# Holding stores behind a load, joining two sums and reordering products at the start of a fused attention and feed-forward kernel

## The chip, the cores and the metric

The kernel runs on one core of a Trainium2 chip. The metric is device microseconds of one execution. All runs compared here are fast (granted TensorE clock 0.998 to 1.000). PE is TensorE, ACT is ScalarE, DVE is VectorE, POOL is GpSimd, SP is SyncE, which here only issues DMAs. Times "at 47.6 us" count from the first instruction of the profiled execution; the span of a profile is about 1.7 us shorter than the run's measured time. A load "lands" at the time for which the profile shows it complete.

## The reference, cut to what matters

```python
B, H, S, D = 8, 8, 576, 64            # batch, heads, tokens, head size
kv  = einsum('bhsd,bhse->bhde', k, v)
out = einsum('bhsd,bhde->bhse', q, kv)
out = out / sqrt(mean(out*out, -1) + 1e-6) * g_norm
x   = out.transpose(0, 2, 1, 3).reshape(4608, 512)
a, b = x @ w_a, x @ w_b               # 512 -> 1536
return (a * b) @ w_out                # 1536 -> 512
```

All inputs are float32 in HBM. The loads that POOL issues cast to bfloat16.

## The kernel before

The 4608 tokens are worked off in nine strips of 512. A strip's feed-forward part is twelve units, each with a product for a and one for b (four matmuls each), then four output groups of 128 tokens. Attention of batch 0 is done at the start, that of batch 1 between the output groups of strip 0, that of batch n+1 inside strip n. The parts that matter:

```python
def load_late(b):                      # batch 2 and later, issued by POOL
    # ... (a gate against qT's earlier use, for b > 2)
    for hs in (slice(0, NP), slice(NP, H)):
        nc.gpsimd.dma_start(out=d[:, hs, :], in_=q[b, hs]...)   # q to a bf16 scratch qs
    load_heads(b, kt[b % NB], k, slice(0, H))
    load_heads(b, vt[b % NB], v, slice(0, H))

def transpose_q(b):                    # issued by SP
    nc.sync.dma_start_transpose(qT[b % 2], qs_d[b])

def o_out(s, g, i):                    # an output group: PSUM -> o_sb -> HBM
    # ... copy by ACT or DVE into t = o_sb[n % 4]
    store(s * STRIP + g * 128, t, 0, d_model)      # SP, two DMAs as a rule

# order of POOL's loads: batch 0; w_a, w_b; w_out; batch 1 pair by pair; batch 2
    for p in range(NP):
        load_pair(1, p)                # q, k, v of two heads
    load_late(2)

# strip 0's output groups and batch 1's attention
    ffn_o(0, 0, X[0])
    pieces = [(1, h1), (1, h2), (2, h1), (2, h2), (3, h1), (3, h2)]
    for n, (g, fcs) in enumerate(pieces):
        o_mm(0, g, O, fcs)
        if fcs is h2:
            o_out(0, g, O)
        # ... sums, x of earlier pairs
        if n < NP:
            A.qtr(n, 2)                # transpose q of pair n on PE
            A.kv1(n, 2)                # k-v product of pair n: needs kt, vt of pair n
        # ...
    transpose_q(2)
```

Inside strip 1, after unit 4, stands the k-v product of batch 2 (`A.kv`, 48 small matmuls); it needs batch 2's k and v:

```python
def slot(A, s, n):
    k0, kn, xs = (4, 1, (6, 9, 11, 13)) if s < 3 else (2, 1, (4, 7, 10, 12))
    # k-v product after unit k0; x of pair p after unit xs[p]
```

PE works its products off in program order here, so one whose v has not landed holds up what stands behind it (in the run gate_only below it waits 0.82 us, and the next unit starts only after it, at 60.99 us). SP does the same with its DMAs: behind the gate of the change the first store went out at 47.84 us, not at 39.15.

Of the kernel before, what the change touches and what calls it, by code (L numbers as in the profile page):

```python
# [9 lines left out]
BF16 = mybir.dt.bfloat16  # L10
# [5 lines left out]
def kernel(  # L16
# [11 lines left out]
    nc = tc.nc  # L28

    B, H, S, D = q.shape  # L30
# [4 lines left out]
    FC = d_ff // 128  # L35
# [6 lines left out]
    EC, EP = 6, 96  # L42
    EARLY = 2
    KORD = tuple(range(KC))
# [4 lines left out]
    def sb(shape, dt, name):  # L49
        return pool.tile(shape, dt, name=name, tag=name)  # L50

    wa_t = sb([128, KC, d_ff], BF16, "wa_t")
    wb_t = sb([128, KC, d_ff], BF16, "wb_t")
# [7 lines left out]
    vt = [sb([EP, H, EC, D], BF16, f"vt{i}") for i in range(NB)]  # L61
# [27 lines left out]
    O = 3  # L89

    qs_d = {b: tc.dram_tile([S, d_model], BF16, name=f"qs{b}") for b in range(EARLY, B)}

    ctx.enter_context(tc.manual_schedule())

# [129 lines left out]
    class Unit:  # L224
# [19 lines left out]
            self.mm(wa_t, kcs)  # L244
            self.mm(wb_t, kcs)

        def rest(self, kcs=KORD):
            self.mm(wa_t, kcs)
            nc.scalar.copy(self.t, self.a)  # L249
            self.mm(wb_t, kcs)  # L250
            nc.vector.tensor_mul(abt[self.s % 2][self.fc], self.b, self.t)  # L251

    n_ab = [0]

    def ffn_ab(s, fc):
        i = n_ab[0]
        n_ab[0] += 2
        Unit(s, fc, i % 3, (i + 1) % 3).rest()
# [18 lines left out]
    def o_mm(s, g, i, fcs, e0=0, e1=d_model):  # L277
        for fc in fcs:
            nc.tensor.matmul(  # L279
                P[:, i, e0:e1],  # L280
                lhsT=abt[s % 2][fc][:, g * 128 : (g + 1) * 128],
                rhs=wo_t[:, fc, e0:e1],
                start=(fc == 0),
                stop=(fc == FC - 1),
            )

    def o_out(s, g, i):
        n = n_o[0]
        n_o[0] += 1
        t = o_sb[n % 4]  # L290
        if n % 2:
            nc.scalar.copy(t, P[:, i, :])  # L292
        else:
            nc.vector.tensor_copy(t, P[:, i, :])  # L294
        store(s * STRIP + g * 128, t, 0, d_model)

    def ffn_o(s, g, i=O):
        o_mm(s, g, i, range(FC))
        o_out(s, g, i)


    def dummy(n, i, cols=STRIP):
        for _ in range(n):
            nc.tensor.matmul(
                P[:, i, 0:cols], lhsT=zeros[:, 0:128], rhs=zeros[:, 0:cols], start=True, stop=True
            )
# [54 lines left out]
    for p in range(1, NP):  # L361
        i = X[p % 2]
        A.kv1(p, 3 - p % 2)
        A.kv1_out(p, 3 - p % 2, nc.vector.tensor_copy)
        A.pss(p - 1, SS)
        if p < NP - 1:
            dummy(1, 2 + p % 2)
            A.qtr(p + 1, 3 - p % 2)
            A.qtr_out(p + 1, 3 - p % 2)
            A.pst(p - 1, X[(p - 1) % 2])  # L370
            A.px(p, i)
            A.psq(p, i)
            dummy(1 if p == 1 else 2, 2 + p % 2)
# [5 lines left out]
    u1 = Unit(0, 1, 4, 5)  # L379
    u0.first((0, 1))  # L380
    A.pss(3, SS, (0,))
    A.pst(3, X[1], (0,))
    u1.first((0, 1))
    A.pss(3, SS, (1,))
    A.pst(3, X[1], (1,))
    u0.first((2,))
    u1.first((2,))
    u0.rest((3,))
    u1.rest((3,))
    for fc in range(2, FC):  # L390
        ffn_ab(0, fc)


    A = Attn(1)
    h1, h2 = range(0, FC // 2), range(FC // 2, FC)
    ffn_o(0, 0, X[0])
    pieces = [(1, h1), (1, h2), (2, h1), (2, h2), (3, h1), (3, h2)]
    for n, (g, fcs) in enumerate(pieces):
# [16 lines left out]
    u1 = Unit(1, 1, 4, 5)  # L415
# [89 lines left out]
```

## Time and profile before

| What | Value |
|---|---|
| time, median of 6 runs | 323.04 us (322.75 to 323.34) |
| span of the profile | 321.4 us |
| PE busy | 98% |
| start step of 512-column matmuls | 0.216 us |
| PE stalls after 17.6 us | 0.32 us at 44.9, 0.28 us at 47.7 |

From the page of the kernel before: span, busy time of the engines, and the chain that ended last.

```profile
span 321.4 us, 4834 instructions
...
PE 315.2 (98%) x1946; PEld 151.2 (47%) x1946; DVE 123.7 (38%) x214; ACT 125.4 (39%) x216; POOL 60.3 (19%) x82
...
PE 84%; DMA 9%; POOL 4%; issue 1%; ACT 0%; POOLq 0%
```

The chain of waits of the kernel before, from 38 to 62 us (start, duration, what):

```profile
39.98 0.63 POOL kt L97
40.61 0.11 issue
40.72 6.89 DMA vt<-in_v_dram
47.62 0.04 issue
47.66 0.38 PE P L138 x12
...
51.47 8.63 PE P L235 x40
60.10 0.88 PE P L138 x48
```

The last load of batch 1's v, issued at 40.72 us, lands at 47.62 us, and what ends last hangs on it. Before it the chain is made of loads and of POOL's issuing them, after it of PE alone. So there are two regimes: up to 47.6 us the loads set the pace, from then on PE does. A PE bar that is 98% busy doesn't tell of this; the chain does.

The timeline of PE (start, duration, instruction, in brackets idle time and what ended it) and of SP's queue, kernel before:

```profile
17.52 0.38 PE L235 MATMUL P<-xt,wa_t 128*128 128x512 bf16 x1 [0.28 <-DVE xt L203]
...
44.89 0.38 PE L138 MATMUL P<-vt,kt 96*64 96x64 bf16 x12 [0.16 <-DMA vt<-in_v_dram]
...
47.66 0.38 PE L138 MATMUL P<-vt,kt 96*64 96x64 bf16 x12
...
60.03 0.95 PE L138 MATMUL P<-vt,kt 96*64 96x64 bf16 x48
```

```profile
39.15 13.50 SPq L272 DMA_DIRECT2D out_dram<-osb  x8
52.83 6.48 SPq L125 DMA_TRANSPOSE qT<-qs  x1
```

The brackets count from the modelled end of the matmul before, so they are smaller than the true loss. I take the loss from start-to-start steps: the one at 44.89 costs 0.32 us, the one at 47.66 (no bracket at all) 0.28 us, the one at 17.52 0.44 us. The line at 60.03 us is batch 2's product: it did not wait, since its v had landed at 59.46 us.

### The profile page before, as it was taken

Reading aid. Unit: us, or ns where it says so; the run is one execution under the profiler, and the core shown is the slowest. Engines: PE = TensorE matmul, PEld = TensorE weight load, DVE = VectorE, ACT = ScalarE, POOL = GpSimd, SP = SyncE. Lnnn points to the kernel's source line nnn. Section 1 sums busy time; section 2 is a strip of 40 time slices with the busy share of each in tenths; the row PEclk is TensorE's granted clock in tenths of the full one; section 3 lists DMA queues with packets and bytes.
Section 4 is the critical chain, followed back from the end, with each engine's and each line's share of the span. In section 5 each row is a group of like instructions: output and inputs, shape, how many; then the busy total and the mean of one; then the engine's idle time right before and its main releaser. Section 6 shows DMA issues by size and latency. Waiting matters only on the chain.

```text
span 321.4 us, 4834 instructions
## 1 busy us (share of the span) xinstructions
PE 315.2 (98%) x1946; PEld 151.2 (47%) x1946; DVE 123.7 (38%) x214; ACT 125.4 (39%) x216; POOL 60.3 (19%) x82
## 2 busy tenths in 40 slices
PE   7999999999999999999999999999999999999995
PEld 3444454444444444444444445444444444444443
DVE  3543344344234423452244423532354243313421
ACT  3643155453345433552355325433453233123310
POOL 8854970330041230500050000000000000000000
PEclk9999999999999999999999999999999999999999
DMA  8999999796369899693598152003000200020002
GB/s 177 197 196 199 199 219 217 115 144 108 94 95 159 121 168 228 64 168 86 140 98 125 65 90 50 2 33 99 2 0 0 100 33 0 26 91 18 0 35 98
DMA packets 69899, 32.61 MB, mean 101 GB/s; under 512 B 43636, under 2 KB 65396, under 8 KB 69876
## 3 DMA queue, kind: packets, MB, share of 16 engines
q0 software_dynamic: 49712, 18.44, 48.7%
q1 hardware_dynamic: 19808, 13.44, 16.2%
q10 hardware_dynamic: 356, 0.43, 0.5%
q8 instruction: 15, 0.25, 0.3%
q14 instruction: 8, 0.07, 0.1%
HBM read 37.75 MB, written 12.98 MB: 158 GB/s over the span
## 4 chain that ended last, share of the span: by engine, by line
PE 84%; DMA 9%; POOL 4%; issue 1%; ACT 0%; POOLq 0%
PE P L235 52%; PE P L279 27%; DMA wb_t<-in_moe_w_b_dram 6%; DMA vt<-in_v_dram 2%; PE P L189 2%; PE P L215 2%; PE P L138 2%; DMA qt<-in_q_dram 2%; POOL wo_t L112 1%; POOL qt L97 1%; POOL kt L97 1%; POOL vt L97 1%; POOL wa_t L332 0%; POOL wb_t L332 0%; POOL wa_t L108 0%
## 5 line engine op out<-in xcount | busy, mean ns | idle before, releaser
L251 DVE TENSOR_TENSOR ab<-P,asb 128x512 bf16<-128x512 f32 x108 | 74.5, 691 | 124.1 <-PE P L235 123.1
L235 PE MATMUL P<-xt,wa_t 128*128 128x512 bf16 x432 | 111.9, 379 | 0.3 <-DVE xt L203 0.3
L235 PE MATMUL P<-xt,wb_t 128*128 128x512 bf16 x432 | 111.8, 379 | 0.0
L279 PE MATMUL P<-wo_t,ab 128*128 128x512 bf16 (+1 forms) x444 | 97.9, 373 | 0.0
L249 ACT CAST asb<-P 128x512 bf16<-128x512 f32 x108 | 63.0, 585 | 81.5 <-PE P L235 80.0
L235 PEld LDWEIGHTS <-wb_t 128*128 128x128 bf16 x432 | 42.3, 98 | 51.4 <-issue 0.6
L279 PEld LDWEIGHTS <-ab 128*128 128x128 bf16 x444 | 43.1, 98 | 45.6
L235 PEld LDWEIGHTS <-wa_t 128*128 128x128 bf16 x432 | 41.7, 98 | 44.2 <-issue 0.2
L203 DVE SCALAR_TENSOR_TENSOR xt<-P,g_col,rs 128x288 bf16<-128x288 f32 x64 | 30.2, 513 | 25.0 <-ACT rs L193 25.0
L193 ACT ACTIVATE rs<-P,eps_t 128x576 f32<-128x576 f32 (+1 forms) x33 | 24.0, 727 | 22.4 <-PE P L189 18.4
L292 ACT COPY osb<-P 128x512 f32<-128x512 f32 x17 | 9.9, 585 | 48.6 <-PE P L279 46.8
L185 ACT ACTIVATE sq<-P 128x576 bf16<-128x576 f32 x31 | 20.2, 650 | 20.0 <-PE P L215 18.0
L294 DVE COPY osb<-P 128x512 f32<-128x512 f32 x18 | 12.4, 691 | 32.8 <-PE P L279 32.8
L120 POOL DMA_DIRECT2D qs<-in_q_dram x12 | 19.5, 1633 | 1.8 <-issue 1.7
L117 POOL COPY gate<-qT 1x1 bf16<-1x1 bf16 x5 | 0.9, 177 | 92.4 <-DMA qT<-qs 92.4
L189 PE MATMUL P<-sq,ones 128*128 128x288 bf16 x64 | 13.3, 286 | 0.5 <-ACT sq L185 0.4
L215 PE MATMUL P<-qT,kvb 128*128 128x288 bf16 x56 | 11.7, 286 | 0.0
L149 ACT CAST kvb<-P 64x256 bf16<-64x256 f32 (+1 forms) x20 | 6.0, 301 | 11.8 <-PE P L138 11.7
L189 PEld LDWEIGHTS <-ones 128*128 128x128 bf16 x64 | 6.2, 98 | 7.5 <-issue 0.4
L138 PEld LDWEIGHTS <-kt 96*64 96x64 bf16 x384 | 7.4, 112 | 4.3 <-issue 3.9
L97 POOL DMA_DIRECT2D vt<-in_v_dram x13 | 9.1, 697 | 0.7 <-DMA qt<-in_q_dram 0.5
L97 POOL DMA_DIRECT2D kt<-in_k_dram x13 | 9.1, 704 | 0.1
(41 smaller groups left out, 65.5 us busy)
## 6 DMA issues: line engine op xcount, KB each, us to landing
out_dram<-osb SPq DMA_DIRECT2D x23, 256.0 KB, 2.0
qs<-in_q_dram POOLq DMA_DIRECT2D x12, 288.0 KB, 6.6
kt<-in_k_dram POOLq DMA_DIRECT2D x6, 576.0 KB, 8.4
vt<-in_v_dram POOLq DMA_DIRECT2D x6, 576.0 KB, 11.0
out_dram<-osb SPq DMA_DIRECT2D x13, 128.0 KB, 2.3
wo_t<-in_moe_w_out_dram POOLq DMA_DIRECT2D x12, 128.0 KB, 6.0
wa_t<-in_moe_w_a_dram POOLq DMA_DIRECT2D x5, 256.0 KB, 9.3
wb_t<-in_moe_w_b_dram POOLq DMA_DIRECT2D x5, 256.0 KB, 9.9
```

The lines of the kernel that those rows point to most:

```text
L97: nc.gpsimd.dma_start(out=t[:, hs, :, :], in_=src[b, hs].rearrange("h (t c) d -> t h c d", c=EC))
L120: nc.gpsimd.dma_start(out=d[:, hs, :], in_=q[b, hs].rearrange("h t d -> t h d"))
L138: nc.tensor.matmul(o[j * D : (j + 1) * D, :], lhsT=kt[self.b % NB][:, 2 * p + j, c, :], rhs=vt[self.b % NB][:, 2 * p + j, c, :], start=(c ...
L185: nc.scalar.activation(sq[p % 3], P[:, i0 : i0 + 2, 0:HF], AF.Square)
L189: nc.tensor.matmul(P[:, i0 + h, 0:HF], lhsT=ones, rhs=sq[p % 3][:, h, :], start=True, stop=True)
L193: nc.scalar.activation(rs[p % 3][:, h0:h1, :], P[:, i0 + h0 : i0 + h1, 0:HF], AF.Abs_reciprocal_sqrt, bias=eps_t,)
L203: nc.vector.scalar_tensor_tensor(out=xt[p][:, t0 : t0 + HF], in0=P[:, x0 + h, 0:HF], scalar=g_col, in1=rs[p % 3][:, h, :], op0=ALU.mult, o ...
L215: nc.tensor.matmul(P[:, i0 + h, 0:HF], lhsT=kvb[self.b % 2][:, p, :], rhs=self.qT[:, p, h * HF : (h + 1) * HF], start=True, stop=True,)
L235: nc.tensor.matmul(self.a if w is wa_t else self.b, lhsT=w[:, kc, self.fc * 128 : (self.fc + 1) * 128], rhs=xt[kc][:, t0 : t0 + STRIP], st ...
L249: nc.scalar.copy(self.t, self.a)
L251: nc.vector.tensor_mul(abt[self.s % 2][self.fc], self.b, self.t)
L279: nc.tensor.matmul(P[:, i, e0:e1], lhsT=abt[s % 2][fc][:, g * 128 : (g + 1) * 128], rhs=wo_t[:, fc, e0:e1], start=(fc == 0), stop=(fc == F ...
```

## The change

The intent: (1) keep the stores of strip 0 from competing with the loads of batch 1, by putting a one-element store ("the gate") that reads the last element of batch 1's last v load ahead of them on SP; (2) put the two halves' sums of pair 3 close together, so that the second half is not late; (3) do a of units 2 and 3 before their b, since w_b lands later; (4) drop a filler matmul (`dummy`, which multiplies zeros).

In the code `kc` counts the four chunks of 128 that the 512 channels of x are cut into. The weights of units 0 and 1 are loaded two chunks at a time, so their w_b comes as one load for kc 0-1, below "the first w_b chunk", and one for kc 2-3. `pss` sums the squares on PE and takes the reciprocal root on ACT, `pst` scales to x on DVE.

```diff
+    gate_d = tc.dram_tile([1, 1], BF16, name="gate_d")
...
         if p < NP - 1:
-            dummy(1, 2 + p % 2)
+            if p == 1:
+                dummy(1, 2 + p % 2)
...
     u0.first((0, 1))
     A.pss(3, SS, (0,))
     A.pst(3, X[1], (0,))
-    u1.first((0, 1))
+    u1.mm(wa_t, (0,))
     A.pss(3, SS, (1,))
     A.pst(3, X[1], (1,))
+    u1.mm(wa_t, (1,))
+    u1.mm(wb_t, (0, 1))
     u0.first((2,))
     u1.first((2,))
     u0.rest((3,))
     u1.rest((3,))
-    for fc in range(2, FC):
+
+    u2 = Unit(0, 2, 0, 1)
+    u3 = Unit(0, 3, 2, 0)
+    u2.part_a()
+    u3.part_a()
+    u2.part_b()
+    u3.part_b()
+    n_ab[0] = 1
+    for fc in range(4, FC):
         ffn_ab(0, fc)
...
+    nc.sync.dma_start(out=gate_d, in_=vt[1][0:1, H - 1, EC - 1, D - 1 : D])
     ffn_o(0, 0, X[0])
```

(`rest` is split into `part_a` and `part_b`; the cut lines only do that.)

More of the change, by code (lines that the diff above doesn't have):

```diff
@@ L245, in first, with part_a, part_b, rest @@
             self.mm(wb_t, kcs)
-        def rest(self, kcs=KORD):
+        def part_a(self, kcs=KORD):
             self.mm(wa_t, kcs)
             nc.scalar.copy(self.t, self.a)
+        def part_b(self, kcs=KORD):
             self.mm(wb_t, kcs)
             nc.vector.tensor_mul(abt[self.s % 2][self.fc], self.b, self.t)
+        def rest(self, kcs=KORD):
+            self.part_a(kcs)
+            self.part_b(kcs)
     n_ab = [0]
```

## The prediction

> **What bounds the kernel now.** The page gives PE 98% busy of a 321.4 us span; in the timeline 512-column matmuls start every 0.216 us. After 17.6 us PE stalls only twice: at 44.89 us (0.32 us) and 47.66 us (0.28 us), when the k-v product of batch 1's pairs 2 and 3 waits for v (landings 44.85 and 47.62 us). The chain of waits agrees: up to 47.6 us it runs through POOL's DMA issues and landings, afterwards through PE alone. So until 47.6 us loads are the bound and PE has small slack; afterwards PE bounds.
>
> **What the change does.**
> 1. *Removed dummy (p = 2).* 0.21 us, because the square/rsqrt chain on ScalarE has about that slack.
> 2. *Sums of pair 3 together.* PE idled 0.44 us before 17.52 us: the second half's sum was issued at 16.09, its rsqrt ended 16.91, its scaling 17.47 us. One matmul instead of four between the sums brings that sum some 0.65 us forward; the wait goes, but the w_b chunk for kc 2-3, landing 16.26 us, then bites for about 0.1 us. Estimate: the last quarter of units 0 and 1 starts near 17.05 us, not 17.52.
> 3. *a of units 2, 3 before b.* w_b for unit 2 lands at 18.91 us and would stall the advanced PE by about 0.25 us; after the swap it is needed near 19.6. Cost: unit 4's a reuses unit 2's b bank one product group (0.86 us) after it, while its 0.69 us multiply with hand-over takes about 1.0 us: 0.15 us lost. Net at unit 4: 0.3 us ahead.
> 4. *Gate.* A one-element store waits for batch 1's last v load, so the two stores of strip 0's first two token groups (issued 39.15 to 42.9 us, 512 KB) cannot move beside the loads. The Trainium skill ("DMA: Bandwidth & Descriptors", Issuing engines are not separate DMA queues) says that transfers from all issuers interleave on the same 16 engines. This trace agrees: load traffic fell from 195 to 130-140 KB/us at 42-44 us while stores moved 115-137; load landings slipped from 0.74 us apart to 1.0-1.3.
>
> **On the critical path.** The 0.3 us of the first part is mostly absorbed: pair 0's v lands at 39.70 us whatever PE does, pair 0's product started at 39.90, so only 0.16 us survives; pair 1 (41.95 against 42.11) leaves 0.12. With stores held, v of pairs 2 and 3 should land near 44.15 and 46.4 us, both waits vanish, and pair 3's product starts near 46.9 instead of 47.66: 0.75 us ahead. But the bytes are only postponed: the stores now meet batch 2's loads. Its v landed at 59.46 us and its product started at 60.03, so if that landing stays put, only about 0.5 us remains. PE carries the rest to the end.
>
> **Prediction:** 322.6 us (0.5 us, 0.15%, less), range 322.0 to 323.2. Faster by over 2%: 0.01; within: 0.98; slower: 0.01.
>
> **Right if:** no PE gap near 17.5; pair 0's product waits for v at about 39.7 us; pair 3's v lands before 46.7 us; no store issue between 39 and 46 us; PE shows no wait at pairs 2 and 3; batch 2's product starts 59.3 to 59.6 us, possibly waiting for v.
>
> **Wrong if:** the released stores and the transpose of batch 2's q delay batch 2's v beyond 60.0 us (then same or slower); landings shift between runs by more than the 0.1-0.2 us margins.

## The result, and the profile after

The changed kernel took 323.32 us, median of 6 runs (322.45 to 324.26); before took 323.04 (322.75 to 323.34). The ratio is 1.0011, with a 95% interval of 0.9992 to 1.0031: the same. (Ratios here are the mean time of one kernel's fast runs over that of the other's of the same rounds, so not quite the ratio of the medians.) The predicted 322.6 us and its range, up to 323.2, were missed. Mark the scatter too: 1.8 us against 0.6 us.

The page after:

```profile
span 322.5 us, 4835 instructions
...
PE 80%; DMA 14%; POOL 4%; issue 1%; ACT 0%; POOLq 0%
```

The chain of waits after, up to 80 us, and the timelines of PE and SP's queue:

```profile
45.35 0.77 POOL kt L99
46.12 15.04 DMA vt<-in_v_dram
61.15 0.04 issue
61.20 0.95 PE P L140 x48
```

```profile
15.71 0.60 PE L237 MATMUL P<-xt,wb_t 128*128 128x512 bf16 x2 [1.05 <-DMA wb_t<-in_moe_w_b_dram]
...
45.32 0.36 PE L140 MATMUL P<-vt,kt 96*64 96x64 bf16 x12
...
47.78 0.35 PE L140 MATMUL P<-vt,kt 96*64 96x64 bf16 x12
...
61.20 0.95 PE L140 MATMUL P<-vt,kt 96*64 96x64 bf16 x48 [1.00 <-DMA vt<-in_v_dram]
```

```profile
47.50 0.29 SPq L416 DMA_DIRECT2D gate_d<-vt  x1
47.84 5.12 SPq L280 DMA_DIRECT2D out_dram<-osb  x8
53.59 6.66 SPq L127 DMA_TRANSPOSE qT<-qs  x1
```

Three things are to be seen. The waits that the change aimed at, at 17.5, 44.9 and 47.7 us, are gone. But the last two are not gone because v came early: in this execution pair 3's v landed at 47.49 us, hardly before the 47.62 of the kernel before, and PE, late by 0.76 us at pair 0 (40.66 against 39.90 us), asked for it only at 47.78. A new wait stands at 15.7 us: the first w_b chunk landed at 15.66 us, not at 14.00. And the load regime now ends at 61.2 us, not at 47.6: the chain hangs on batch 2's v, which landed at 61.15 us instead of 59.46. The product of batch 2 lost 1.07 us start to start (it began 1.38 us after the matmul before it, 0.31 us in the kernel before). The whole difference of the two spans, 322.5 less 321.4, is there: 61.20 less 60.03.

### The profile page after: what moved, and what is told of

It reads as the page before. It is cut to its first block, busy times and chain, and to the rows that moved or that the text cites. A ratio compares the mean times of both kernels' runs of the same rounds, so it can differ in the third digit from the quotient of the medians.

```text
span 322.5 us, 4835 instructions
## 1 busy us (share of the span) xinstructions
PE 315.1 (98%) x1945; PEld 151.1 (47%) x1945; DVE 123.6 (38%) x214; ACT 125.3 (39%) x216; POOL 60.2 (19%) x82
## 4 chain that ended last, share of the span: by engine, by line
PE 80%; DMA 14%; POOL 4%; issue 1%; ACT 0%; POOLq 0%
PE P L237 49%; PE P L287 26%; DMA wb_t<-in_moe_w_b_dram 6%; DMA vt<-in_v_dram 5%; PE P L217 2%; PE P L191 2%; DMA wo_t<-in_moe_w_out_dram 2%; PE P L140 2%; DMA qt<-in_q_dram 2%; POOL qs L122 1%; POOL kt L99 1%; POOL vt L99 1%; POOL qt L99 1%; POOL wa_t L340 0%; POOL wb_t L340 0%
## 5 line engine op out<-in xcount | busy, mean ns | idle before, releaser
L191 PE MATMUL P<-sq,ones 128*128 128x288 bf16 x64 | 13.2, 286 | 0.5 <-ACT sq L187 0.4
L140 PE MATMUL P<-vt,kt 96*64 96x64 bf16 x384 | 8.6, 197 | 1.0 <-DMA vt<-in_v_dram 1.0
```

What stands on the lines that cost most here:

```text
L140: nc.tensor.matmul(o[j * D : (j + 1) * D, :], lhsT=kt[self.b % NB][:, 2 * p + j, c, :], rhs=vt[self.b % NB][:, 2 * p + j, c, :], start=(c ...
L191: nc.tensor.matmul(P[:, i0 + h, 0:HF], lhsT=ones, rhs=sq[p % 3][:, h, :], start=True, stop=True)
```

## The experiments

Theory A: the gate only postpones the stores. All 1 MB of them now meets the load of batch 2, whose v then lands after its product is due. Rival B: the late w_b chunk, a matter of chance, and what follows from it. Rival C: the changed start itself costs time. The table has all runs; "wait" is what the brackets of the PE timeline show at batch 2's product, and "b1 v" and "b2 v" are the landings of the last v load of batches 1 and 2.

| Run | median us (range) | ratio to before, interval | b1 v, us | b2 v, us | wait, us |
|---|---|---|---|---|---|
| again | 323.41 (322.59 to 324.52) | 1.0012, 0.9995 to 1.0028 | 47.59 | 60.83 | 0.55 |
| gate_only | 323.17 (322.46 to 323.63) | 1.0001, 0.9988 to 1.0014 | 46.20 | 60.06 | 0.82 |
| no_gate | 323.03 (322.69 to 323.25) | 0.9999, 0.9987 to 1.0011 | 47.47 | 59.54 | none |
| late_slot | 324.08 (323.79 to 324.32) | 1.0031, 1.0019 to 1.0043 | 46.29 | 60.49 | none |
| late2 | 322.55 (322.15 to 323.26) | 0.9985, 0.9972 to 0.9998 | 46.31 | 59.29 | none |
| gate_late2 | 322.82 (322.56 to 323.44) | 0.9997, 0.9983 to 1.0011 | 46.39 | 60.03 | none |
| gate2 | 322.45 (322.41 to 323.01) | 0.9984, 0.9972 to 0.9997 | 46.35 | 56.43 | none |
| hold_transpose | 323.59 (323.26 to 323.68) | 1.0013, 1.0000 to 1.0027 | 46.22 | 59.51 | 0.22 |
| before_late2 | 323.25 (322.84 to 323.57) | 1.0002, 0.9990 to 1.0014 | 47.60 | 59.94 | none |
| after_gate2 | 322.35 (322.22 to 322.75) | 0.9976, 0.9963 to 0.9989 | 46.34 | 56.73 | none |
| again2 | 322.63 (322.36 to 323.79) | 0.9991, 0.9972 to 1.0009 | 46.41 | 59.67 | 0.32 |
| before_again | 323.03 (322.50 to 323.12) | 0.9993, 0.9978 to 1.0007 | 47.53 | 59.47 | none |
| wb_late_after | 323.48 (323.35 to 324.03) | 1.0015, 1.0002 to 1.0029 | 46.37 | 59.95 | none |
| wb_late_before | 323.60 (323.19 to 324.06) | 1.0016, 1.0003 to 1.0028 | 47.10 | 59.07 | none |

None of these differences comes near 2%. The intervals tell more, but among fourteen of them one that misses 1 by a hair (late2, gate2) proves little by itself. Each trace is one execution.

### The changed kernel again, and its two halves

`again` has no edit. `gate_only` is the kernel before with the two gate lines of the diff; `no_gate` is the changed kernel without them.

> The changed kernel once more, unaltered. Theory A (the gate moves 1 MB of stores into the load of batch 2, so that batch 2's v lands after its product is due): v of batch 2 lands later than 60.3 us again and PE stands about 0.3 to 1.2 us before the product of strip 1; time within 0.5 us of before, spread over 1 us. Rival B (chance: in the profiled run the first w_b chunk happened to land at 15.66 us instead of 14.00 and everything after it is a consequence): with w_b landing near 14.0 the PE wait at 15.7 is gone, v of batch 2 lands near 59.5, and the time is 0.5 us or more under before.

> The kernel before with nothing but the gate. Theory A: v of batch 2 lands at 60.3 to 61.5 us and PE waits for it; batch 1's pairs 2 and 3 do not wait; time equal to before or up to 0.7 us above. Rival B (gate harmless and useful): batch 1's last v at 46.4 us, batch 2's v near 59.5 us, time 0.3 to 0.6 us under before.

> The changed kernel without the gate: only the start is changed. Theory A: v of batch 2 lands near 59.5 us and the product of strip 1 does not wait, batch 1's pairs 2 and 3 wait for v as before; time 0 to 0.3 us under before, since loads absorb what the start gains. Rival C (the changed start itself costs time, PE waiting for the first w_b chunk): time above before, with the loss still there at 47 us.

The PE timelines of no_gate and of gate_only, and gate_only's SP queue:

```profile
39.73 0.38 PE L139 MATMUL P<-vt,kt 96*64 96x64 bf16 x12
...
44.91 0.38 PE L139 MATMUL P<-vt,kt 96*64 96x64 bf16 x12 [0.30 <-DMA vt<-in_v_dram]
...
59.88 0.95 PE L139 MATMUL P<-vt,kt 96*64 96x64 bf16 x48
```

```profile
46.87 0.35 PE L139 MATMUL P<-vt,kt 96*64 96x64 bf16 x12
...
60.11 0.95 PE L139 MATMUL P<-vt,kt 96*64 96x64 bf16 x48 [0.82 <-DMA vt<-in_v_dram]
```

```profile
46.22 0.29 SPq L397 DMA_DIRECT2D gate_d<-vt  x1
46.55 5.58 SPq L273 DMA_DIRECT2D out_dram<-osb  x8
53.73 6.24 SPq L126 DMA_TRANSPOSE qT<-qs  x1
```

The gate does what it was made for: batch 1's v lands at 46.20 us and pair 3's product starts at 46.87 us, 0.79 us ahead of before's 47.66. At batch 2's product all of it has been given back: 60.11 us against 60.03, as v landed at 60.06 (theory A had asked for 60.3 or later). Time: unchanged. In no_gate the stalls at 44.9 us are back, batch 2's product doesn't wait, and pair 0's product waits for its v, as predicted: it starts at 39.73 us, v having landed at 39.69. Batch 2's product starts at 59.88 us, 0.15 us ahead of before, and the time shows nothing of that size. So rival C falls for the start as such, and theory A holds in gate_only without any late w_b chunk (there it landed at 13.77 us). In again that chunk was late once more (15.62 us), and the v of both batches too. Rival B's test was therefore not made by this run; again2 makes it below.

Where the head start goes can be counted in the trace's DMA packets, in KB (loads counted at bfloat16 size, "SP and ACT" holding stores and the transpose):

| Window, us | before: loads | before: SP and ACT | gate_only: loads | gate_only: SP and ACT |
|---|---|---|---|---|
| 39 to 46.5 | 1250 | 385 | 1412 | 0 |
| 46.5 to 55 | 1325 | 401 | 1146 | 670 |
| sum | 2575 | 786 | 2558 | 670 |

By 55 us both kernels have loaded the same to within 17 KB. The loads' gain of 162 KB is spent again as the stores pass. That the issuers share the same DMA engines is what the Trainium skill states ("DMA: Bandwidth & Descriptors", Issuing engines are not separate DMA queues), and here it cuts both ways.

### A later place for the product

```diff
     k0, kn, xs = (4, 1, (6, 9, 11, 13)) if s < 3 else (2, 1, (4, 7, 10, 12))
+    if s == 1:
+        k0, kn, xs = 6, 1, (8, 10, 12, 14)      # late_slot, on the changed kernel
+        k0, kn, xs = 6, 1, (7, 9, 11, 13)       # late2, gate_late2, before_late2
```

The two lines are alternatives.

> The changed kernel with the product of batch 2 placed two units (3.45 us) later in strip 1, and what follows from it 2, 1, 1, 1 units later; no instruction is added. Theory A: the wait for batch 2's v is gone, whatever its landing, and the time falls to 322.0 to 322.6 us, some 0.5 to 1.1 us under before. Rival B or C: the time stays where the changed kernel's is, within 0.2 us.

This one failed, and by my edit. The wait at batch 2's product is gone, but the last x of batch 2 now comes so late in strip 1 that strip 2 waits for it. PE timeline of late_slot:

```profile
86.83 0.38 PE L237 MATMUL P<-xt,wa_t 128*128 128x512 bf16 x1 [1.40 <-DVE xt L205]
```

The time went up to 324.08 us. A product moved away from a wait needs room behind it as well. late2 repairs that on the changed kernel; gate_late2 is gate_only and before_late2 is the kernel before with the same edit.

> The changed kernel with batch 2's product two units later as in late_slot, but what follows it at units 7, 9, 11, 13 in place of 8, 10, 12, 14, so that strip 2 has its x in time. Theory A (batch 2's v lands at 60 to 61.2 us because of the held stores, and that wait is all that the gate costs): no wait at batch 2's product (62 to 63 us), no wait at 86.8 us as in late_slot, time 322.1 to 322.7, under before by 0.4 to 1.0 us. If another wait replaces it (x or transpose late), it shows as a PE gap between 62 and 90 us and the time stays at 323 or above.

> The gate alone with the same later product. Theory A: as late2, 322.1 to 322.6 us. It also tells what the changed start is worth under the gate: if late2 and this one agree within 0.2 us, nothing; if in late2's profile the first w_b chunk lands near 15.6 us and its time is 0.5 us or more above this one, the start costs.

> Control for late2: the kernel before, no gate, with only the later place of batch 2's product. Theory A: nothing waited there, so nothing is gained: 322.8 to 323.3 us, within 0.2 us of before, with the waits at 44.9 and 47.7 us still there. Rival (the later place is a gain by itself): 0.4 us or more under before.

In late2 no wait is left after 40 us, and 322.55 us is faster than before, if only by 0.15% (the interval ends at 0.9998). But in its profile v landed at 59.29 us, not at the 60 to 61.2 expected, so the later place saved hardly anything in that execution. The control before_late2 gains nothing, as theory A demands: where nothing waited, moving the product is worth nothing. gate_late2 missed its range: its profile has no wait at batch 2's product and a span of 320.8 us, 0.6 us under before's, but its timed runs reach from 322.56 to 323.44 us, and their ratio of 0.9997 is no gain beyond doubt. This I leave unexplained; the two kernels together don't show that moving the product wins the lost time back.

### Another place for the stores

```diff
 def o_out(s, g, i):
     ...
-    store(s * STRIP + g * 128, t, 0, d_model)
+    if s:
+        store(s * STRIP + g * 128, t, 0, d_model)
+    else:
+        held.append((g * 128, t))
...
     transpose_q(2)
+    nc.sync.dma_start(out=gate_d, in_=vt[2][0:1, H - 1, EC - 1, D - 1 : D])
+    for t0, t in held:
+        store(t0, t, 0, d_model)
```

gate2 is the kernel before with this edit. after_gate2 is the changed kernel with it, in place of its own gate.

> The kernel before, with all stores of strip 0 held until batch 2's v (not batch 1's) has landed, the transpose of batch 2's q issued ahead of them; the product stays at its place. Theory A: batch 2's v lands at 57 to 58.5 us, PE waits neither at 44 to 48 nor at 59 to 60 us, time 322.1 to 322.6. Against theory A: v still lands at 60 us or later with no store beside it, and the time stays within 0.2 us of before.

> The changed kernel (its start and all) with the gate on batch 2's v and the transpose ahead, as in gate2. Theory A: v of batch 2 before 58.5 us, no wait at 44 to 60 us; batch 1's pair 3 product at 46.85 us; about 0.15 us under gate2, 322.2 to 322.5 us. If the first w_b chunk lands near 15.6 us in this run, PE waits 1.0 to 1.2 us there, pair 3's product starts near 47.8 and the time is 323 or more.

SP's queue and PE in gate2:

```profile
50.55 5.84 SPq L126 DMA_TRANSPOSE qT<-qs  x1
56.45 0.45 SPq L419 DMA_DIRECT2D gate_d<-vt  x1
56.95 5.75 SPq L273 DMA_DIRECT2D out_dram<-osb  x8
```

```profile
47.02 0.35 PE L139 MATMUL P<-vt,kt 96*64 96x64 bf16 x12
...
59.37 0.95 PE L139 MATMUL P<-vt,kt 96*64 96x64 bf16 x48
```

With the stores out of the way of batch 2's loads as well, its v lands at 56.43 us instead of 60.06 in gate_only, the product starts at 59.37 us without a wait, and the time is 322.45 us. This is theory A's strongest test: the same bytes, but released later (the gate now waits for batch 2's v, and the transpose goes ahead of the stores). after_gate2 adds the changed start and is the fastest kernel, 322.35 us (ratio 0.9976, interval 0.9963 to 0.9989). That it is 0.10 us under gate2 compares medians of different rounds and settles nothing. Its profiled execution began slow (first k-v product at 7.71 us, against 7.14 in before), so pair 3's product started at 47.17 us, not at the 46.85 expected. The chain on its page runs through PE from start to end, and no load stands in it:

```profile
PE 98%; issue 1%; ACT 1%; DVE 0%
PE P L237 58%; PE P L288 29%; PE P L191 3%; PE P L217 2%; PE P L316 2%; PE P L140 2%; PE P L164 1%; PE P L178 0%; ACT sq L187 0%; ACT o_end L500 0%; PE P L369 0%; DVE zeros L327 0%; DVE eps_t L331 0%
```

### Stores or transpose?

In gate_only the transpose of batch 2's q also overlaps with the end of v's load. hold_transpose is gate_only with one line:

```diff
+    nc.sync.dma_start(out=gate_d, in_=vt[2][0:1, H - 1, EC - 1, D - 1 : D])
     transpose_q(2)
```

> The gate alone, and the transpose of batch 2's q held until batch 2's v has landed. If the overlap with the transpose makes v late (theory A2): v lands at 59.4 us or earlier against 60.06 in gate_only, and the product's wait shrinks to under 0.3 us. If the stores alone do (theory A1): v lands at 59.8 us or later. The time itself may rise, as the transpose then lands late for x.

v landed at 59.51 us, between the two thresholds, and the other kernels with the gate have it anywhere from 59.29 us (late2, transpose not held) to 61.15. So the size of the transpose's share stays open. The stores have the larger one, as gate2 shows: there the transpose ran from 50.55 us on beside the load, without stores, and v landed at 56.43; without the transpose, but with the stores, it landed at 59.51. The price of holding the transpose is plain: it landed at 64.84 us, and x waited for it.

```profile
64.88 0.41 PE L216 MATMUL P<-qT,kvb 128*128 128x288 bf16 x2 [0.81 <-DMA qT<-qs]
```

### Chance and the first w_b chunk

again2 is the changed kernel and before_again the kernel before, both unaltered.

> The changed kernel a third time, to see how often the first w_b chunk lands late. If its lateness belongs to the changed start: near 15.6 us again. If it is chance: near 14.0, batch 1's last v at 46.3 and batch 2's v near 60 us, with a PE wait of 0.8 to 1.0 us there, span about 321.3 us. In either case PE waits at batch 2's product.

> The kernel before once more, for a second trace. First w_b chunk at 14.0 us, waits at 44.9 and 47.7 us, batch 2's v near 59.5 us with no wait; if the first w_b chunk is late by chance here too, it lands near 15.6 us and PE waits about 1 us before 15.7 us, while batch 1's pair 3 starts within 0.4 us of 47.66. Time within 0.2 us of before.

In again2 the w_b chunk landed at 14.05 us, batch 1's v at 46.41, batch 2's v at 59.67. PE timeline of again2:

```profile
59.71 0.95 PE L140 MATMUL P<-vt,kt 96*64 96x64 bf16 x48 [0.32 <-DMA vt<-in_v_dram]
```

So the same program has at least two courses. In this one the span was 321.0 us and that run took 322.76 us; in the two traces with the late chunk the runs took 324.26 and 323.91 us. Over all its 16 timed runs the changed kernel was at 323.79 us or more five times; the kernel before was so twice in 50. Rival B is thus right that chance added to the profiled run, and theory A is right that a wait for batch 2's v is there even in the good course, though at 0.32 us a smaller one than the 0.8 to 1.0 expected. before_again repeats before.

Does the late chunk cause the late loads? The last pair forces it, by loading the first chunks in the order w_a, w_a, w_b, w_b:

```diff
-    for c in range(0, KC, 2):
-        for w, src in ((wa_t, wa_v), (wb_t, wb_v)):
+    for w, src in ((wa_t, wa_v), (wb_t, wb_v)):
+        for c in range(0, KC, 2):
```

> The changed kernel with the first four weight chunks loaded in the order w_a, w_a, w_b, w_b in place of w_a, w_b, w_a, w_b, so that the first w_b chunk lands near 15.8 us in every run, as it did by chance in two of three traces of the changed kernel. Theory D (a late w_b makes PE late, and that in turn makes the later loads late): PE waits about 1.2 us before 15.8 us, batch 1's last v lands at 47.4 to 47.6 us, batch 2's v at 60.8 us or later, time 323.7 to 324.3 us. Rival E (late loads are a chance of their own): batch 1's last v still lands at 46.2 to 46.5 us, batch 2's v at 59.6 to 60.1, time 322.6 to 323.3 us.

> The same exchange in the kernel before. Theory D: PE waits about 1 us before 15.8 us and is 0.5 us or more late at 35.6 us; since PE had 0.6 us of waits to give up at 44 to 48 us, batch 1's pair 3 starts at 47.7 to 48.1 us, batch 2's v does not hold PE up, and the time is 0 to 0.5 us above before, so less than the changed kernel loses. If its loads become late as well: v of batch 2 at 60.5 us or later and 0.7 us or more above before.

The PE timeline of wb_late_after:

```profile
15.96 0.60 PE L237 MATMUL P<-xt,wb_t 128*128 128x512 bf16 x2 [0.87 <-DMA wb_t<-in_moe_w_b_dram]
...
60.38 0.95 PE L140 MATMUL P<-vt,kt 96*64 96x64 bf16 x48
```

Theory D falls. With the chunk late on purpose batch 1's v lands at 46.37 us and batch 2's at 59.95, as on a good day. Against the kernel before of the same rounds (323.10 us) both are slower by about the same, 0.4 and 0.5 us by the medians, where D had the kernel before lose less; rival E's range, up to 323.3 us, was missed too. (Both profiled executions also started slow, with the first k-v product at 7.57 and 7.80 us instead of 7.14, so I take the timings and not the spans.) A late chunk costs something of its own, but does not make the later loads late. That all the loads were 1.1 to 1.2 us late by 47.5 us in the two slow traces has another cause, which stays open. It came about well after the w_b chunk: pair 0's v was 0.1 and 0.3 us later than in again2 (39.88 and 40.04 us against 39.74), pair 2's 1.1 and 1.2 us (45.26 and 45.38 against 44.19).

## Why the prediction was wrong

1. *Right: the two regimes, and loads as the bound up to 47.6 us.* no_gate shows it: the start ahead, pair 0's product held at 39.73 us (39.7 predicted), nothing of note gained in time.
2. *Sizes at the start.* In again2 the last quarter of units 0 and 1 began at 16.96 us, not the 17.05 predicted, as the w_b chunk for kc 2-3 didn't hold PE up. Unit 4's a lost 0.15 us, as predicted, and began at 21.43 us, 0.40 us ahead of before's 21.83, where 0.3 was predicted. The filler was worth less than the 0.21 us said: in the profile after, the first unit began at 14.05 us against 14.19.
3. *Right: the gate's effect on batch 1.* v of pair 3 landed at 46.20 to 46.41 us in seven of nine traces with the gate (46.4 predicted), and pair 3's product started at 46.87 us in gate_only (46.9 predicted). The other two traces are of the changed kernel itself, in its slow course: 47.49 and 47.59 us, so there this step failed as well.
4. *Wrong: "if that landing stays put".* This is the step that failed. I had seen that the stores would meet batch 2's loads, but took the landing of its v, 59.46 us, as fixed and counted 0.5 us as kept. In the nine traces with that gate it landed at 59.29 to 61.15 us, mean 60.1; in the five without a gate at 59.07 to 59.94, mean 59.5. PE, 0.7 to 0.8 us ahead, needed it at about 59.2. In gate_only nothing remained of 0.79 us, in again2 0.32 us, in the profile after less than nothing. My own list of what would make it wrong had this landing beyond 60.0 us; I gave it too little weight. When the stores were kept out of that load too, in gate2, the gain came: 0.51 us by the medians.
5. *Wrong: landings of one trace, the first w_b chunk at 14.00 us among them, as fixed times.* The prediction doesn't name this chunk, and has shifting landings only in its list of what would make it wrong. In every trace there is a gap in the landings of 1.4 to 2.3 us that begins between 13.4 and 14.1 us. In before the chunk lands just ahead of it; in two of three traces of the changed kernel just behind it. The range of 322.0 to 323.2 us had no room for a second course of the program at 323.8 to 324.5 us. The eleven other runs of the changed kernel have a median of 322.79 us, inside the range. Runs sorted by their own time are no test, but how much of the missed median is due to this step, and how much to step 4, stays open; gate_only, which lost its gain without a late chunk, shows step 4 by itself.

## What to carry to other kernels

When transfers are held back so that urgent ones pass, ask what the held ones will meet on release, and what slack the next urgent load has: here it was 0.57 us, and PE running 0.8 us ahead had used it up before the delay came. Release them where the queue is free for long (here after batch 2's v: 322.45 and 322.35 us, against 322.96 and 323.08 for the kernel before in the same rounds), or move the consumer too, leaving room behind it. Where gains are a few tenths of a microsecond take several traces of the same program: a landing time read from one trace is one draw.

## What the Trainium skill lacked or had wrong

- "DMA: Bandwidth & Descriptors", Issuing engines are not separate DMA queues: right as far as it goes, but without a price. Here 385 KB of stores went with 162 KB less loaded in 7.5 us (1250 against 1412 KB), and the loads lost it again on release (1325 against 1146 KB in the next 8.5 us).
- "DMA: Bandwidth & Descriptors", Anatomy of one DMA — SWDGE, puts a DMA at about 2.0 us plus bytes over 436 GB/s. That is an estimate of 2.6 us for a w_out chunk (256 KB read as float32); with other loads queued, these took 4.97 to 9.73 us from issue to landing in the profile after. No page says how to estimate a landing in a filled queue.
- "Runtime: NRT & Kernel Launch", Instruction fetch mechanics, calls the cost of crossing a 16 KiB boundary of the instructions "one DMA tail-bump, mostly hidden". Every trace here has a 16,384-byte packet of the instruction queue at 13.2 to 14.1 us, taking 0.9 us, and the landing gap of 1.4 to 2.3 us lies beside it. Whether one causes the other no run shows; no page has it.
- No page says that a program's DMA landings can take two courses: the same kernel had the last v of batch 1 at 46.41 us in one trace and at 47.49 and 47.59 us in two others.
